# Routing noise loaded into its place, the ranking of unit 0 in later chunks, and another order of the second layer's products

## The chip, the cores and the metric

The kernel runs on one core of one Trainium2 chip. The metric is the device time of one execution in microseconds; the median of three runs is compared.

## The reference

Two blocks follow each other. First a gated linear attention over 4 x 8 heads of 768 steps with 48 features, then a router that sends each of the 3072 tokens (384 features) to 2 of 8 experts:

```python
for t in range(S):                                  # per batch and head
    state = alpha[t][:, None] * state + outer(k[t], v[t])
    y[t] = q[t] @ state
x = y, heads side by side                           # (3072, 384)
noisy = x @ w_gate + log1p(exp(x @ w_noise)) * noise
top2 = the two largest of the 8; w = softmax over the two
for e in range(8):                                  # w1[e] 384x1024, w2[e] 1024x384
    out[rows of e] += w * (relu(x[rows] @ w1[e]) @ w2[e])
```

All of it is in 32-bit floating point.

## The kernel before

**Chunks.** The attention runs over 24 chunks of 128 tokens, six to a batch entry. The main loop over n writes the order of the work out by hand: one iteration issues 15 pieces, which are numbered by place. Place 0 issues loads on SP (values of chunk n+2, alpha of n+5, keys and queries of n+4) and the store of chunk n-2. Then come keys (1), inverses (2), alphas (3), turn_y (4), turn_k (5), scaled (6), queries (7), block (8), output (9), no_more (10), state (11), scores (12), masked (13) and products (14). They belong to different chunks: keys, inverses, scaled and queries to n+2, alphas and products to n+3, turn_k, state, scores and masked to n+1, output and block to n, turn_y to n-1. Every engine works its own instructions off in that order.

**What hangs together in a chunk.** TensorE transposes keys and alphas (L347), turns the output rows (L281), turns the keys (L438, left out ahead of the last chunk of a batch entry), transposes the queries (L347), and multiplies output (L470, L258), state (L453) and scores (L426). All transposes share two banks in turn (the pool `tp`), so a transpose waits until the tile two before it has been copied out. ScalarE copies out keys, alphas, rows, blocks and outputs (L474). VectorE scans the running products (L375, tile `P_all`, one buffer) and the inverses (L387, tile `over`, one buffer), multiplies the queries (L415) and masks the scores (L431). GpSimd multiplies the keys (L405, `scaled`), copies the last column of `P_all` (L416, in the piece queries) and scales the state (L456). A new `P_all` is written only after the copy L416 of the one before.

**Routing.** A unit is six chunks; there are four. `routing` is a generator whose steps are s1 logits and exp, s2 ln, s3 the noise multiplied in (L706), s4 to s6 the two largest of two chunks each (L711, L712), with the choice and the exponential of the gates behind s6 (L729), s7 the rest of the choice and the running counts (L735 to L758, mostly GpSimd), s8 the ranks (TensorE, L763, L764), s9 the places of the table's entries. `ROUTE[u]` lists when the step is taken: (d, place) of unit u is the iteration n = d + 6(u + 1) - 1. So (3, 8) of unit 0 is n = 8 and (3, 13) of unit 1 is n = 14. Step s9 queues twelve entries, and the last thing of each iteration, `put_some(3)`, issues three of them as indirect DMAs on GpSimd (L172). The routing of units 2 and 3 lies in the second phase.

**Noise.** The noise (3072 x 8) is loaded by one DMA on SP as 24 rows of 4 KB (L236), turned by eight transposes on TensorE in iteration 2 (L242) and copied by ScalarE into its place (L243).

**Pairs.** The second phase takes 24 pairs of 128-row tiles, a pair belonging to one expert. Each has 11 products of the first layer (L1219) and 7 of the second (L1226), with sums of blocks on VectorE (`hx`, `wt`) that save products. Steps carry a time; they are sorted by it. The table of rows is read (`tab`, SP) after the entries of units 0 and 1 have been put, then the rows are gathered (L950, GpSimd). `ending` holds the end of a pair, `last_ending` that of the last. The results C and D share one bank, A and B have their own; D is `hs[1][1]` times `wt[3]`, C is `hs[1][0]` times a block of the weights, B starts with `hx[0]` times `wt[0]`.

Of the kernel before, what the change touches and what calls it, by code (L numbers as in the profile page):

```python
# [9 lines left out]
F32 = mybir.dt.float32  # L10
# [9 lines left out]
def kernel(  # L20
# [32 lines left out]
    nc = tc.nc  # L53
    B, H, S, D = q.shape
    N, DM = out.shape
    E, _, F = moe_w1.shape
    C = 128
# [173 lines left out]
                out=to_rows.rearrange("p (j o) c -> p j o c", o=2)[:, :, odd, ds((1 - odd) * 2 * D, 2 * E)],  # L231
                in_=w_r.rearrange("p (j o) w e -> p j o (w e)", o=2)[:, :, odd])

    def load_noise(on):
        by_chunk = on["two"].tile([C, KO * F], F32, tag="w1", name="by_chunk")[0:NT, 0:C * E]
        nc.sync.dma_start(out=by_chunk, in_=moe_noise.rearrange("(n p) e -> n (p e)", p=C))  # L236
        return by_chunk.rearrange("n (p e) -> n e p", e=E)

    def turn_noise(by_chunk, on):
        tp = on["tp"].tile([C, E, NT], F32, tag="tp", name="tp")  # L240
        for e in range(E):
            nc.tensor.transpose(tp[:, e, :], by_chunk[:, e, :], ident[0:NT, 0:NT])  # L242
        nc.scalar.copy(noise.rearrange("p n e -> p e n"), tp)  # L243


    def few(on, shape, name, late=False):
# [51 lines left out]
    def fast_gla(on):  # L298
# [184 lines left out]

        ROUTE = (((1, 8), (2, 8), (2, 10), (2, 11), (3, 4), (3, 8), (3, 10), (4, 12), (5, 0)), ((1, 9), (2, 8), (2, 10), (3, 1), (3, 4), (3, 11), (3, 13), (5, 0), (5, 11), (5, 12)))
        routes = [routing(u, on) for u in range(NU)]

        def route(n, place):
# [570 lines left out]
    def pairs(on):  # L1060
# [161 lines left out]
        def product2(name, H, W, new=False):  # L1222
            if new:
                open_bank(name)
            for f in range(FO // 2):
                nc.tensor.matmul(bank[name], H[:, f, :], W[:, f, :], start=new and f == 0, stop=True,  # L1226
                                 skip_group_check=True)
# [8 lines left out]
        def scaled(i, s, half, name):  # L1236
            nc.scalar.activation(o[:, s, half], bank[name], AF.Copy, scale=gate(i, s))  # L1237

        def added(i, s, half, name, to=None):
            to = o if to is None else to  # L1240
            nc.vector.scalar_tensor_tensor(to[:, s, half], bank[name], gate(i, s), to[:, s, half], op0=ALU.mult, op1=ALU.add)  # L1241
# [62 lines left out]
        def steps(i):  # L1304
# [36 lines left out]
                (10.0, lambda: less(hx[3], hs[1][0], hx[1])),  # L1341
                (10.1, lambda: less(hx[2], hs[0][0], hs[0][1])),
                (10.55, lambda: product2("A", hs[0][0], v(0, 0), True)),
                (11.9, lambda: product2("B", hx[0], wt[0], True)),
                (11.95, lambda: scaled(i, 0, LEFT, "A")),
                (13.2, lambda: product2("C", hs[1][0], v(1, 0), True)),
                (13.25, lambda: scaled(i, 1, RIGHT, "B")),
                (14.6, lambda: product2("A", hx[1], wt[1])),
                (15.95, lambda: scaled(i, 0, RIGHT, "A")),
                (6.5 if i == 5 else 8.5 + late + after, lambda: get_prev(i)),  # L1350
# [1 line left out]

        def ending(i, v, summing):
            return (
                (15.9, lambda: product2("D", hs[1][1], wt[3])),
                (17.3, lambda: product2("B", hx[3], v(1, 1))),
                (17.35, lambda: (added(i, 0, LEFT, "C"), scaled(i, 1, LEFT, "D"))),
                (18.6, lambda: product2("A", hx[2], wt[2])),
                (18.65, lambda: added(i, 0, RIGHT, "B")),
                (20.0 - 0.05, lambda: added_to_both(i, 1, "A")),  # L1360
                (summing, lambda: combine(i)),
                (summing + 1.3, lambda: put_pair(i)))

        def last_ending(i, v, summing):
            rows = prev[i % 2]
            return (
                (14.7, lambda: added(i, 0, LEFT, "C")),
                (15.9, lambda: product2("B", hx[3], v(1, 1))),
                (16.0, lambda: with_prev(i, 1, RIGHT)),
                (17.3, lambda: product2("A", hx[2], wt[2])),  # L1370
                (17.35, lambda: (added(i, 0, RIGHT, "B"), with_prev(i, 0, BOTH), put_half(i, 0))),
                (18.6, lambda: product2("D", hs[1][1], wt[3])),
                (18.65, lambda: (scaled(i, 1, LEFT, "A"), added(i, 1, RIGHT, "A", rows), with_prev(i, 1, LEFT))),
                (20.0, lambda: added(i, 1, LEFT, "D", rows)),
                (20.0, lambda: put_half(i, 1)))
# [103 lines left out]
    with ExitStack() as es:  # L1479
# [31 lines left out]
                work.pop(0)[1]()  # L1511

        held = []
        NOISE_AT = 5
        FIRST_ORDER = "scores masked inverses keys scaled turn_k queries output block state alphas no_more turn_y products"
        ORDER = "keys inverses alphas turn_y turn_k scaled queries block output no_more state scores masked products"

# [4 lines left out]
        with tc.manual_schedule():  # L1522
# [28 lines left out]
            alphas(2)  # L1551
            no_more(1)
            load(4, "a")
            held.append(load_noise(on))
            state(0)
            products(2)
            no_more(2)
            for n in range(LAST):
                pieces = {"keys": lambda: keys(n + 2), "inverses": lambda: inverses(n + 2),
                          "scaled": lambda: scaled_keys(n + 2), "alphas": lambda: alphas(n + 3),  # L1560
                          "turn_y": lambda: turn_y(n - 1), "turn_k": lambda: turn_k(n + 1),
                          "queries": lambda: queries(n + 2), "products": lambda: products(n + 3),
                          "no_more": lambda: no_more(n + 3), "block": lambda: block(n), "output": lambda: output(n),
                          "state": lambda: state(n + 1), "scores": lambda: scores(n + 1),
                          "masked": lambda: masked(n + 1)}
                names = (FIRST_ORDER if n == 0 else ORDER).split()
                assert sorted(names) == sorted(pieces)
                pieces = [lambda: (load_v(n + 2), load(n + 5, "a"), load(n + 4, "kq"), put_y(n - 2))] + \
                    [pieces[name] for name in names]
                chunk = [lambda piece=piece, place=place: (piece(), route(n, place)) for place, piece in enumerate(pieces)]  # L1570
                last = [lambda: put_some(3)]
                if n == 0:
                    chunk.append(lambda: place_router(held.pop(0)))
                if n == 1:
                    last.append(lambda: held.append(nothing_in(on["two"])))
                if n == 2:
                    chunk.append(lambda: clear_table(held.pop()))
                if n == 2:
                    last.append(lambda: (clear_pairs(), clear_halves()))
                if n == 3:  # L1580
                    last.append(place_slots)
                if n == 2:
                    chunk.insert(NOISE_AT, lambda: turn_noise(held.pop(0), on))
                for at, place, t in ((16, 9, -410.0), (15, 9, -409.0), (14, 9, -408.0), (8, 9, -405.0), (7, 9, -404.0), (6, 9, -403.0), (5, 9, -402.0), (3, 9, -300.0), (2, 1, -199.0), (1, 1, -101.0), (1, 14, -100.5), (1, -1, -100.0)):
                    if n == LAST - at:
                        chunk.insert(place, lambda t=t: until(t))
                for piece in chunk + last:
                    piece()
# [46 lines left out]
```

## Time and profile before

| | |
|---|---|
| median of 3 runs | 653.38 us (653.23 to 654.1) |
| profiled execution | 653.14 us, of which the span from the first to the last instruction is 651.1 us |
| TensorE (matmul), VectorE, ScalarE, GpSimd busy | 98%, 71%, 48%, 47% of the span |
| granted TensorE clock | 0.997 of full speed |

In a timeline a row is one or several merged instructions: start, duration, engine, line, operation, tiles, count, and in brackets how long the engine was idle before it and who ended that. Ends of matmuls are modelled, so what a stretch of TensorE cost is read from the distance of starts. The chunk of iteration n begins with the eight transposes of L347 (keys, alphas); iteration 2 begins at 29.07 us, iteration 8 at 66.94 us, iteration 16 at 118.36 us.

### The profile page before, as it was taken

To read this page: it belongs to the slowest core of one execution; us is meant where nothing else is said; L and a number is where in the kernel's file an instruction comes from. 1 tells how busy PE (TensorE), PEld (TensorE's weight loads), DVE (VectorE), ACT (ScalarE), POOL (GpSimd) and SP (SyncE) were. 2 spreads that over 40 slices of the span, in tenths; PEclk is the share of its full clock that TensorE was granted. 3 is DMA by queue.
4 is the path that set the end of the run, shared out by engine and by line. 5 is a ranking of instruction groups with operands and counts; after the bars stand their busy time and mean duration, and the time that the engine had idled before them with its cause. 6 is when DMAs were issued, how large, how long until landed. Compare 5 with 4: busy or idle time off the path is not lost. (4 is left out here: it accounts for less than half of the span.)

```text
span 651.1 us, 14753 instructions
## 1 busy us (share of the span) xinstructions
PE 637.3 (98%) x5509; PEld 614.4 (94%) x5509; DVE 461.0 (71%) x1045; ACT 310.9 (48%) x624; POOL 309.1 (47%) x407
## 2 busy tenths in 40 slices
PE   8999999999999999999999999999999999999994
PEld 6899999998999999999999999999999999998894
DVE  6778889887779888777677777567574665746532
ACT  3767778675554454433434433434334444334430
POOL 6362577784343577774353542513445044450231
PEclk9999999999999999999999999999999999999998
DMA  9999998973766676665366298943899439993011
GB/s 140 173 213 161 231 190 160 222 160 109 244 191 218 204 214 197 205 220 119 87 168 173 83 223 235 209 151 89 215 260 221 145 109 215 260 264 103 32 53 46
DMA packets 170260, 112.52 MB, mean 173 GB/s; under 512 B 135095, under 2 KB 157362, under 8 KB 170180
## 3 DMA queue, kind: packets, MB, share of 16 engines
q1 hardware_dynamic: 132340, 33.20, 30.0%
q10 hardware_dynamic: 26112, 54.30, 27.7%
q0 software_dynamic: 11728, 23.99, 12.6%
q8 instruction: 46, 0.75, 0.5%
q14 instruction: 34, 0.28, 0.1%
HBM read 95.09 MB, written 15.37 MB: 170 GB/s over the span
## 5 line engine op out<-in xcount | busy, mean ns | idle before, releaser
L942 POOL DMA_INDIRECT out_dram<-prev,where x48 | 58.1, 1210 | 164.5 <-DVE prev L1254 144.2
L1219 PE MATMUL sc<-xs,ws 128*128 128x128 f32 x576 | 78.2, 279 | 0.0
L1230 ACT ACTIVATE h<-h 128x512 f32<-128x512 f32 x72 | 45.2, 631 | 66.3 <-DVE h L1163 63.4
L1219 PE MATMUL sc<-xt,w 128*128 128x128 f32 x576 | 75.1, 275 | 0.5 <-ACT xt L1152 0.5
L950 POOL DMA_INDIRECT x_in<-x_rows,where x48 | 52.4, 1091 | 44.7 <-issue 29.1
L1219 PEld LDWEIGHTS sc<-xt,w 128*128 128x128 f32 x576 | 70.5, 192 | 0.8 <-ACT xt L1152 0.8
L1219 PEld LDWEIGHTS sc<-xs,ws 128*128 128x128 f32 x576 | 70.0, 192 | 0.8 <-issue 0.2
L1226 PE MATMUL o_ps<-wt,hx 128*128 128x192 f32 x384 | 70.2, 326 | 0.0
L931 POOL DMA_INDIRECT prev<-out_dram,where x48 | 52.1, 1085 | 36.2 <-DMA out_dram<-prev_half,where_half 16.6
L1163 DVE TENSOR_TENSOR h<-sc,m 128x512 f32<-128x512 f32 x48 | 33.2, 691 | 47.1 <-PE sc L1219 44.4
L1226 PEld LDWEIGHTS o_ps<-wt,hx 128*128 128x128 f32 x384 | 63.7, 190 | 0.0
L172 POOL DMA_INDIRECT table<-entry,place_u x48 | 54.2, 1130 | 15.2 <-issue 12.1
L1219 PE MATMUL h_ps<-xt,w 128*128 128x128 f32 x384 | 50.7, 275 | 0.0
L1237 ACT ACTIVATE o<-o_ps,tab 128x192 f32<-128x192 f32 x49 | 20.6, 420 | 59.2 <-PE o_ps L1226 58.5
L1241 DVE SCALAR_TENSOR_TENSOR o<-h_ps,tab,o 128x192 f32<-128x192 f32 x48 | 20.0, 416 | 38.9 <-PE h_ps L1226 38.2
L1219 PE MATMUL sc<-xs,w 128*128 128x128 f32 x384 | 46.8, 275 | 0.0
L1219 PEld LDWEIGHTS h_ps<-xt,w 128*128 128x128 f32 x384 | 46.7, 192 | 0.0
L405 POOL TENSOR_TENSOR k_P<-k_P,over 128x512 f32<-128x512 f32 (+1 forms) x25 | 28.9, 1159 | 37.2 <-DVE over L387 31.5
L347 PE MATMUL tp<-ident,ins 128*128 128x128 f32 x288 | 44.3, 290 | 1.6 <-DMA ins<-in_alpha_dram 0.5
L1219 PEld LDWEIGHTS sc<-xs,w 128*128 128x128 f32 x384 | 44.8, 192 | 0.0
L347 PEld LDWEIGHTS tp<-ident,ins 128*128 128x128 f32 x288 | 33.5, 148 | 6.7 <-issue 1.6
L1237 ACT ACTIVATE o<-h_ps,tab 128x192 f32<-128x192 f32 x47 | 19.9, 422 | 39.8 <-DVE o L1241 31.1
(262 smaller groups left out, 1442.7 us busy)
## 6 DMA issues: line engine op xcount, KB each, us to landing
w<-in_moe_w_dram ACTq DMA_DIRECT2D x42, 512.0 KB
w<-in_moe_w_dram ACTq DMA_DIRECT2D x56, 384.0 KB
ins<-in_alpha_dram SPq DMA_DIRECT2D x24, 192.0 KB
ins<-in_k_dram SPq DMA_DIRECT2D x24, 192.0 KB
ins<-in_q_dram SPq DMA_DIRECT2D x24, 192.0 KB
vt<-in_v_dram SPq DMA_DIRECT2D x24, 192.0 KB
x_rows<-y_sb SPq DMA_DIRECT2D x24, 192.0 KB
ins<-in_moe_w_dram ACTq DMA_DIRECT2D x9, 512.0 KB
```

The lines of the kernel that those rows point to most:

```text
L172: put = nc.gpsimd.indirect_dma_start(out=table, out_offset=bass.IndirectOffsetOnAxis(ap=place, axis=0), in_=entry, in_offset=None, bounds_ ...
L347: nc.tensor.transpose(tp[:, j, :], src[:, 2 * j:2 * j + 2, :], ident)
L405: nc.gpsimd.tensor_tensor(c["k"][:, at], c["k"][:, at], over[:, at, 1:CB], op=ALU.mult)
L931: get = nc.gpsimd.indirect_dma_start(out=rows.bitcast(U32), out_offset=None, in_=out.bitcast(U32), in_offset=bass.IndirectOffsetOnAxis(ap= ...
L942: put = nc.gpsimd.indirect_dma_start(out=out, out_offset=bass.IndirectOffsetOnAxis(ap=at, axis=0), in_=rows, in_offset=None, bounds_check= ...
L950: nc.gpsimd.indirect_dma_start(out=rows, out_offset=None, in_=x_rows[0:units * UT, :], in_offset=bass.IndirectOffsetOnAxis(ap=at, axis=0), ...
L1163: nc.vector.tensor_tensor(to, p, q, op=ALU.add)
L1219: nc.tensor.matmul(bank[name][:, f, :], W[:, ds(f * C, C)], X, start=new and f == 0, stop=True, skip_group_check=True)
L1226: nc.tensor.matmul(bank[name], H[:, f, :], W[:, f, :], start=new and f == 0, stop=True, skip_group_check=True)
L1230: nc.scalar.activation(t, t if src is None else src, AF.Relu)
L1237: nc.scalar.activation(o[:, s, half], bank[name], AF.Copy, scale=gate(i, s))
L1241: nc.vector.scalar_tensor_tensor(to[:, s, half], bank[name], gate(i, s), to[:, s, half], op0=ALU.mult, op1=ALU.add)
```

## The change

Three parts. The noise is loaded per unit by four DMAs of 768 runs of 32 bytes straight into its tile, in iterations 3, 8, 13 and 18, behind place 0; the transposes and the copy are gone. In `ROUTE`, steps s6 to s9 of unit 0 move one iteration later, and step s4 of unit 1 moves from place 1 of iteration 14 to place 11 of iteration 13. In a pair the order of the second layer's products A, B, C, A, D, B, A becomes A, D, B, A, C, B, A: D now opens the bank that it shares with C, and the scaling of B's first half is 1.4 later. The last pair keeps the old order.

```diff
-    def load_noise(on):
-        by_chunk = on["two"].tile([C, KO * F], F32, tag="w1", name="by_chunk")[0:NT, 0:C * E]
-        nc.sync.dma_start(out=by_chunk, in_=moe_noise.rearrange("(n p) e -> n (p e)", p=C))
-        return by_chunk.rearrange("n (p e) -> n e p", e=E)
-
-    def turn_noise(by_chunk, on):
-        tp = on["tp"].tile([C, E, NT], F32, tag="tp", name="tp")
-        for e in range(E):
-            nc.tensor.transpose(tp[:, e, :], by_chunk[:, e, :], ident[0:NT, 0:NT])
-        nc.scalar.copy(noise.rearrange("p n e -> p e n"), tp)
+    def load_noise(u):
+        nc.sync.dma_start(out=noise[:, ds(u * UC, UC)], in_=moe_noise[ds(u * UT, UT), :].rearrange("(n p) e -> p n e", p=C))
...
-        ROUTE = (((1, 8), (2, 8), (2, 10), (2, 11), (3, 4), (3, 8), (3, 10), (4, 12), (5, 0)), ((1, 9), (2, 8), (2, 10), (3, 1), (3, 4), (3, 11), (3, 13), (5, 0), (5, 11), (5, 12)))
+        ROUTE = (((1, 8), (2, 8), (2, 10), (2, 11), (3, 4), (4, 8), (4, 10), (5, 12), (6, 0)), ((1, 9), (2, 8), (2, 10), (2, 11), (3, 4), (3, 11), (3, 13), (5, 0), (5, 11), (5, 12)))
...
-                (11.9, lambda: product2("B", hx[0], wt[0], True)),
                 (11.95, lambda: scaled(i, 0, LEFT, "A")),
-                (13.2, lambda: product2("C", hs[1][0], v(1, 0), True)),
-                (13.25, lambda: scaled(i, 1, RIGHT, "B")),
...
         def ending(i, v, summing):
             return (
-                (15.9, lambda: product2("D", hs[1][1], wt[3])),
+                (11.9, lambda: product2("D", hs[1][1], wt[3], True)),
+                (13.2, lambda: product2("B", hx[0], wt[0], True)),
+                (14.65, lambda: scaled(i, 1, RIGHT, "B")),
+                (15.9, lambda: product2("C", hs[1][0], v(1, 0))),
...
         def last_ending(i, v, summing):
             return (
+                (11.9, lambda: product2("B", hx[0], wt[0], True)),
+                (13.2, lambda: product2("C", hs[1][0], v(1, 0), True)),
+                (13.25, lambda: scaled(i, 1, RIGHT, "B")),
...
-        NOISE_AT = 5
+        NOISE_AT = (3, 8, 13, 18)
...
-            held.append(load_noise(on))
...
-                if n == 2:
-                    chunk.insert(NOISE_AT, lambda: turn_noise(held.pop(0), on))
+                if n in NOISE_AT:
+                    chunk.insert(1, lambda: load_noise(NOISE_AT.index(n)))
```

## Rows read from the trace of the kernel before

**Rows 1.** Page, part 1: busy time, share of the span, instructions.

```profile
PE 637.3 (98%) x5509; PEld 614.4 (94%) x5509; DVE 461.0 (71%) x1045; ACT 310.9 (48%) x624; POOL 309.1 (47%) x407
```

**Rows 2.** Groups by line, TensorE: count, busy us, mean ns, idle before it.

```profile
L1226 PE MATMUL h_ps<-wt,hx 128*128 128x192 f32 x192 | 35.2, 326 | 0.0
```

**Rows 3.** Timeline of TensorE, iterations 2 and 3: start, us, what.

```profile
29.07 1.09 PE L347 MATMUL tp<-ident,ins 128*128 128x128 f32 x8
30.98 1.06 PE L242 MATMUL tp<-ident,by_chunk 24*128 24x24 f32 x8
36.67 1.09 PE L347 MATMUL tp<-ident,ins 128*128 128x128 f32 x8
42.91 1.09 PE L347 MATMUL tp<-ident,ins 128*128 128x128 f32 x8
```

**Rows 4.** Page, part 3: a DMA queue's packets, MB, share of 16 engines; then TensorE's waits.

```profile
q1 hardware_dynamic: 132340, 33.20, 30.0%
PE tp L347 <- DMA ins<-in_alpha_dram: 0.5, 1, 0.5
```

**Rows 5.** Timeline of TensorE, iterations 9 and 10.

```profile
73.17 1.09 PE L347 MATMUL tp<-ident,ins 128*128 128x128 f32 x8
74.59 1.15 PE L281 MATMUL h_ps<-to_rows,yT 128*128 128x112 f32 x8 [0.34 <-ACT yT L474]
80.22 0.42 PE L763 MATMUL h_ps<-chosen,before 128*128 128x48 f32 x2
80.70 1.06 PE L347 MATMUL tp<-ident,ins 128*128 128x128 f32 x8
```

**Rows 6.** Timeline of ScalarE, iterations 8 and 9.

```profile
73.84 0.23 ACT L729 ACTIVATE entry<-entry 128x12 f32<-128x12 f32 x1 [1.56 <-DVE entry L723]
79.69 0.72 ACT L463 COPY S_block<-S 64x192 f32<-64x192 f32 x2 [2.25 <-POOL S L456]
```

**Rows 7.** Timeline of GpSimd, iteration 15, and of VectorE, iterations 15 and 16.

```profile
118.29 1.19 POOL L405 TENSOR_TENSOR k_P<-k_P,over 128x512 f32<-128x512 f32 x1
119.42 0.19 POOL L416 COPY P_end<-P_all 128x4 f32<-128x4 f32 x1
119.64 1.52 DVE L375 TENSOR_TENSOR_SCAN P_all<-shared,least 128x516 f32<-128x516 f32 x1 [0.59 <-POOL P_end L416]
122.56 0.66 DVE L415 TENSOR_TENSOR q_P<-tp,P_all 128x512 f32<-128x512 f32 x1
```

**Rows 8.** GpSimd from 86.5 to 122.5 us: the puts by line, then timeline rows.

```profile
L172 POOL DMA_INDIRECT table<-entry,place_u x12 | 14.3, 1190 | 3.2 <-issue 3.0 <-POOL S L448 0.2
98.75 0.51 POOL L456 TENSOR_TENSOR S<-S,P_end 128x192 f32<-128x192 f32 x1 [0.30 <-DVE S L455]
...
103.32 1.21 POOL L405 TENSOR_TENSOR k_P<-k_P,over 128x512 f32<-128x512 f32 x1
...
108.58 1.70 POOL L172 DMA_INDIRECT table<-entry,place_u  x1 [0.30 <-issue]
```

**Rows 9.** Timeline of TensorE, iterations 15 and 17.

```profile
113.10 0.63 PE L438 MATMUL tp<-ident,k_P 128*128 128x128 f32 x4 [0.20 <-ACT k_P L397]
...
123.91 1.07 PE L347 MATMUL tp<-ident,ins 128*128 128x128 f32 x8
```

**Rows 10.** Timeline ahead of the first pair: GpSimd, VectorE, GpSimd, TensorE.

```profile
146.24 1.17 POOL L172 DMA_INDIRECT table<-entry,place_u  x1 [0.31 <-issue]
152.33 0.17 DVE L1117 TENSOR_SCALAR tab<-tab 128x2 f32<-128x2 f32 x1 [0.75 <-DMA tab<-table]
153.12 1.83 POOL L950 DMA_INDIRECT x_in<-x_rows,where  x1 [3.90 <-DVE where L1128]
160.31 1.16 PE L1219 MATMUL sc<-xt,w 128*128 128x128 f32 x8 [0.54 <-ACT xt L1152]
```

**Rows 11.** Timeline of TensorE, one pair.

```profile
551.20 1.54 PE L1226 MATMUL h_ps<-wt,hx 128*128 128x192 f32 x8
552.58 1.46 PE L1226 MATMUL h_ps<-w,h 128*128 128x192 f32 x8
```

## The prediction

> **What bounds the kernel now.** I read the page first: TensorE's matmuls are busy 98% of the span [rows 1], so a change counts if it takes work from TensorE or changes one of the few places where it waits. The groups by line show where it doesn't wait: the second layer's product that starts B has no idle time ahead of its 192 matmuls [rows 2], and the others look the same. What is left is the chunk phase, where the distance between the first transposes of successive iterations is what an iteration costs. An undisturbed one takes 42.91 - 36.67 = 6.24 us; iteration 2, which turns the noise, takes 36.67 - 29.07 = 7.60 [rows 3]. So I go through the chunk phase queue by queue, and ask of each moved step who is behind it.
>
> **Noise, the gain.** The eight transposes and the copy behind them make iteration 2 longer by 7.60 - 6.24 = 1.36 us [rows 3]. Nothing else of that iteration is late, so all of it should go: -1.36. The lower end is what the eight transposes alone show as busy, 1.06, the upper end 1.4.
>
> **Noise, the cost.** Four loads of 768 packets join SP's queue. The queue's 132340 packets took 30.0% of 16 engines' span of 651.1 us, which is 23.6 ns for one, of 251 bytes in the mean [rows 4]; 768 of them over 16 engines are at most 1.13 us a load. TensorE waited for an input load only at the start, 0.5 us [rows 4], and a load is issued about two iterations, 12 us, before its use; that is the cover, so I take 0. Without it four loads would cost 4 x 1.13 = 4.5. The Trainium skill speaks against such loads (DMA: Bandwidth & Descriptors, the section Measured (HBM→SBUF, 128 partitions, SWDGE, issued from GpSimd)): below 64 KB the count of descriptors decides, at about 10.5 ns a packet. By that a load would be an estimated 0.5 us of the engines, and the sum stays the same as long as the cover holds. SP's issue is one more instruction behind place 0; TensorE, VectorE and ScalarE don't wait for it. The two pieces of weight loading that the insertion moves by one place are SP's too: 0.
>
> **Unit 0, iteration 9.** Iteration 9 takes 80.70 - 73.17 = 7.53 us, of which 80.70 - 80.22 = 0.48 are the rank products and 7.53 - 6.24 - 0.48 = 0.81 are waits, the largest for ScalarE's output copy yT [rows 5]. The cause is one iteration earlier: the gates' exponential of step s6 waits 1.56 us on ScalarE for VectorE, and yT is behind it [rows 6]. With s6 one iteration later, VectorE has only two of the six maxima in each iteration and should reach the gates before TensorE needs yT. The wait goes: -0.81. What is late next: the running counts of s7 (GpSimd) now end in iteration 10, and behind them the scaled state and ScalarE's block copy. That copy was 2.25 us late in iteration 9 before [rows 6]. Iteration 10 has no turned keys and is shorter, so yT of iteration 10 comes out just when it is needed in iteration 11, and the next transposes wait some 0.3 for copies. I take -0.81 + 0.3 = -0.5, with the ends 0 and -0.81. The rank products only change their iteration: 0.
>
> **Unit 0, its puts.** This is the costly part, and it isn't visible in the diff. Step s9 goes from iteration 10 to 11, so the four groups of three puts end iterations 11 to 14 instead of 10 to 13. In iteration 14 unit 1 has its s7, whose counts on GpSimd are last. Before, iteration 14 had no puts, and the scaled keys of the next iteration start right after the counts, at 118.29 [rows 7]. Now a group stands between them. Twelve puts cost 14.3 + 3.2 us, that is 17.5 / 4 = 4.37 a group [rows 8]. The shortest group, from the end of the state's scaling at 98.75 + 0.51 = 99.26 to 103.32, is 4.06; with one put of 1.70 in place of 1.19 it would be 4.9 [rows 8]. I take the mean, since it is the same work on the same queue.
>
> Who waits: behind the puts stand the scaled keys (1.19) and the copy of the last column of `P_all`, which ends at 119.42 + 0.19 = 119.61. VectorE already waits 0.59 us for that copy before it may write the next `P_all` [rows 7]. So VectorE is late by the whole 4.37. Its scans lead to the multiplied queries, which now end at 122.56 + 0.66 = 123.22 [rows 7]. The alphas' transposes of iteration 17 need that bank; they are the second half of the eight that begin at 123.91, so at about 124.36 [rows 9]. The margin is 124.36 - 123.22 = 1.14, and TensorE loses 4.37 - 1.14 = 3.2 us there.
>
> The rest of the 4.37 comes due at the first pair. Unit 1's four groups of puts follow in GpSimd's queue behind the same late inverses, the last ends at 146.24 + 1.17 = 147.41, and from there a chain of waits runs to the first product: the table's read lands and ends VectorE's idle 0.75 at 152.33, GpSimd's gather has waited 3.90 for VectorE's row numbers, and TensorE waits 0.54 for the turned rows at 160.31 [rows 10]. This chain is last there already, so it carries all 4.37 to the pairs: +4.4.
>
> **Unit 1's step s4.** It moves ahead of the masks and scans of iteration 13 in VectorE's queue, but the gates of s6 still have the same work ahead of them. The wait of iteration 15 (0.20 idle and a few tenths around it [rows 9]) stays: 0, at best -0.4.
>
> **Second layer.** The product that starts B takes 552.58 - 551.20 = 1.38 us in one pair instead of 1.30 [rows 11], which is a wait for `hx[0]` of 0.08. With D in its place the wait has 1.3 us more room. `hs[1][1]` and `wt[3]` are made long before. C's sum waited for the whole bank before, that is for D in the fifth place, and now for C in the fifth place: no change. B's scaling comes 1.3 later but has two products until B is written again. So -0.1 in all, and 0 in the other pairs, since TensorE has no wait there to lose [rows 2].
>
> **The sum.** -1.36 - 0.5 + 4.4 + 0 - 0.1 = +2.4. On the profiled execution's own 653.14 us (span 651.1 and 2.04 around it) this is 655.5; the median lies 0.24 above that execution, so 655.8. With all ends one way the forecast itself spans 4.06 - 1.4 - 0.81 - 0.4 - 0.1 = +1.3 to 4.9 - 1.06 - 0 = +3.8, or 654.7 to 657.2.
>
> **Rivals.** (a) The later puts are hidden, and the gains stay: -1.36 - 0.5 - 0.1 = -2.0, 651.4, faster. Place: GpSimd between iterations 14 and 15. It decides if a group delays the scaled keys by less than the margin of 1.14 us. For it speaks that GpSimd is busy only 47% of the span [rows 1]; against it the copy that VectorE already waits for [rows 7]. Chance 0.12. (b) TensorE loses its 3.2 but the chain at the first pair gives the difference back, because puts run faster beside a waiting VectorE or VectorE catches up: 3.2 - 1.36 - 0.5 - 0.1 = +1.2, 654.6, no change that can be told. Chance 0.18. (c) The new order in the pairs makes TensorE wait where it doesn't now, for a bank or a copy that I follow wrongly; at the 0.08 of the one wait that there is, 23 pairs lose 1.8 on top: 657.6. Chance 0.05. (d) The noise loads are not covered, because the input loads run out of lead: 4.5 on top, 660.3; the single 0.5 us wait for a load speaks against it [rows 4]. Chance 0.03. By the Trainium skill's figure above the uncovered loads would be an estimated 4 x 0.5 = 2.0 on top.
>
> **How the numbers follow.** The forecast has 0.62. A measurement of this kernel tells about 0.2% from no change, 1.3 us, so no change is 652.1 to 654.7. Faster is (a): 0.12. No change is most of (b) and the edges: 0.16. Slower is the rest, 0.72. The range leaves out (a) and (d), and with the tails no more than 2 in 10: 653.3 to 657.8.
>
> **What would show it.** Right: iteration 2 as long as iteration 3; three puts on GpSimd right behind the counts of unit 1, the next scaled keys some 4.4 us later against TensorE, VectorE idle over 4 us before the following `P_all`, two waits of TensorE of together about 3 us in iterations 16 and 17; the first product of the pairs some 2.5 us later than 160.31; pair lengths unchanged. Wrong: an iteration 16 of the old length, or waits of TensorE for DMA in the chunk phase, or pairs that are longer or shorter by a tenth each.

## The result, and the profile after

The changed kernel takes 656.58 us, the median of 11 runs (654.9 to 658.57); the kernel before takes 653.29 beside it (11 runs, 651.71 to 654.1). The ratio is 1.0054, with the interval [1.0044, 1.0064]: slower by about 3.5 us. The forecast was 655.8. The profiled execution of after has 658.57 us and a span of 656.7, the slowest of its eleven. Its span is 5.6 longer than that of before (651.1), where the medians differ by 3.3; so a term read from this one trace can be larger than its share of the median.

The page, part 1 (busy time) and the row of part 2 with the clock granted to TensorE in 40 slices:

```profile
PE 639.9 (97%) x5501; PEld 616.9 (94%) x5501; DVE 460.9 (70%) x1045; ACT 312.4 (48%) x623; POOL 310.2 (47%) x407
PEclk9999999899999999999999999999999999999998
```

TensorE has eight matmuls fewer and is busy 2.6 us more [rows 1]. The 8 in the eighth slice is the first hint of why: between 115 and 131 us the granted clock isn't full. In before that digit is a 9.

TensorE's waits in after (line, who released it: us in total, times, longest):

```profile
PE tp L339 <- DVE q_P L407: 1.8, 1, 1.8
...
PE sc L418 <- POOL k_P L397: 1.3, 2, 1.1
...
PE tp L339 <- DMA ins<-in_alpha_dram: 0.5, 1, 0.5
```

The first two are new. The wait for an input load is the 0.5 us that was there before [rows 4], so the noise loads cost TensorE nothing that shows; they landed 2.9 to 3.7 us after their issue.

Cut into iterations (distance from the eight transposes that begin one to those that begin the next, worked out from the timelines of both), the 138.56 us from the start of iteration 1 to the first product of the pairs in before, and the 143.38 in after, lie like this. Iterations that aren't named have 6.23 in both, but for 1 and 4, which are as long in after as in before.

| iteration | 2 | 9 | 10 | 11 | 15 | 16 | 17 | last stretch, to the pairs | sum |
|---|---|---|---|---|---|---|---|---|---|
| before | 7.60 | 7.53 | 5.31 | 6.23 | 7.44 | 5.55 | 6.21 | 11.50 | 138.56 |
| after | 6.23 | 6.23 | 5.82 | 6.60 | 7.58 | 6.67 | 11.14 | 11.91 | 143.38 |
| difference | -1.37 | -1.30 | +0.51 | +0.37 | +0.14 | +1.12 | +4.93 | +0.41 | +4.82 |

From there to the end it is 490.97 us in after and 490.76 in before. Of the other 0.8 of the 5.6, 0.6 lies ahead of iteration 1, which starts at 22.38 instead of 21.75; the kernels of the experiments start it between 20.14 and 22.24, whatever was changed.

**The gains.** TensorE of after, the first transposes of iterations 2, 3 and 4 (as [rows 3]), then of 9, 10, 11 and 12 (as [rows 5]); start, duration, what:

```profile
29.70 1.09 PE L339 MATMUL tp<-ident,ins 128*128 128x128 f32 x8
...
35.93 1.09 PE L339 MATMUL tp<-ident,ins 128*128 128x128 f32 x8
...
42.16 1.09 PE L339 MATMUL tp<-ident,ins 128*128 128x128 f32 x8
```

```profile
72.42 1.09 PE L339 MATMUL tp<-ident,ins 128*128 128x128 f32 x8
...
78.65 1.09 PE L339 MATMUL tp<-ident,ins 128*128 128x128 f32 x8
...
84.47 1.06 PE L339 MATMUL tp<-ident,ins 128*128 128x128 f32 x8
...
91.07 1.09 PE L339 MATMUL tp<-ident,ins 128*128 128x128 f32 x8
```

Iteration 2 is as long as iteration 3. Iteration 9 has lost its waits and its rank products, iteration 10 has the rank products now, and iteration 11 is 0.37 longer.

**The puts.** GpSimd of after, iteration 15: the end of unit 1's counts, the three puts, the scaled keys and the copy of the last column (as [rows 7]):

```profile
117.11 0.20 POOL L750 TENSOR_TENSOR seen<-past,chosen 128x8 f32<-128x8 f32 x1
117.83 1.02 POOL L172 DMA_INDIRECT table<-entry,place_u  x1 [0.52 <-issue]
119.15 0.98 POOL L172 DMA_INDIRECT table<-entry,place_u  x1 [0.30 <-issue]
120.44 0.98 POOL L172 DMA_INDIRECT table<-entry,place_u  x1 [0.30 <-issue]
121.43 1.19 POOL L397 TENSOR_TENSOR k_P<-k_P,over 128x512 f32<-128x512 f32 x1
122.55 0.19 POOL L408 COPY P_end<-P_all 128x4 f32<-128x4 f32 x1
```

From the end of the counts (117.31) to the scaled keys (121.43) the group takes 4.12. VectorE stands meanwhile:

```profile
122.78 1.52 DVE L367 TENSOR_TENSOR_SCAN P_all<-shared,least 128x516 f32<-128x516 f32 x1 [4.75 <-POOL P_end L408]
...
125.70 0.67 DVE L407 TENSOR_TENSOR q_P<-tp,P_all 128x512 f32<-128x512 f32 x1
```

**What TensorE makes of it.** Its timeline from the start of iteration 16 (117.34) over that of 17 (124.01) to that of 18 (135.16):

```profile
117.34 1.06 PE L339 MATMUL tp<-ident,ins 128*128 128x128 f32 x8
...
119.55 1.06 PE L462 MATMUL y<-q_P,S_block 128*128 128x128 f32 x8
120.54 1.09 PE L250 MATMUL y<-shared,vt 128*48 128x128 f32 x16
122.68 1.16 PE L418 MATMUL sc<-q_P,k_P 48*128 48x128 f32 x16 [1.05 <-POOL k_P L397]
...
124.01 0.63 PE L339 MATMUL tp<-ident,ins 128*128 128x128 f32 x4
126.42 1.11 PE L339 MATMUL tp<-ident,ins 128*128 128x128 f32 x4 [1.77 <-DVE q_P L407]
127.33 1.89 PE L273 MATMUL h_ps<-to_rows,yT 128*128 128x112 f32 x8
...
130.71 1.91 PE L462 MATMUL y<-q_P,S_block 128*128 128x128 f32 x8
132.56 1.12 PE L250 MATMUL y<-shared,vt 128*48 128x128 f32 x16
...
135.16 1.09 PE L339 MATMUL tp<-ident,ins 128*128 128x128 f32 x8
```

The two waits that the forecast named are there. But behind the second one no wait follows, and the work still takes nearly twice as long: the output product of iteration 16 runs from 119.55 to 120.54, that of iteration 17 from 130.71 to 132.56, 1.85 for the same eight matmuls. The windows show it. A row has the stretch and its length, then for TensorE's matmuls, its weight loads, VectorE, ScalarE and GpSimd the busy us and the instructions, then the granted clock, the share of the DMA engines and their GB/s. First after, then before over the first two of these stretches:

```profile
117.00:125.80 8.80, 6.51 (x68) 5.78 (x68) 3.98 (x6) 4.49 (x11) 4.97 (x8) 1.00 0.80 167
125.84:132.67 6.83, 6.25 (x30) 6.03 (x32) 5.96 (x13) 2.67 (x7) 5.92 (x9) 0.50 0.86 174
132.70:139.00 6.30, 6.30 (x84) 6.00 (x86) 4.03 (x6) 4.19 (x11) 4.32 (x6) 1.00 0.67 114
```

```profile
117.00:125.80 8.80, 8.67 (x95) 7.99 (x92) 7.90 (x17) 5.42 (x14) 5.54 (x14) 1.00 0.94 195
125.84:132.67 6.83, 6.83 (x88) 6.53 (x87) 5.97 (x9) 4.92 (x14) 5.79 (x7) 1.00 1.05 220
```

For 6.83 us the granted clock is 0.50, the lower of its two levels (1.2 instead of 2.4 GHz), and TensorE gets 30 matmuls done where before had 88 (in part others, and shorter ones). Ahead of it TensorE was busy 6.51 of 8.80 us. Iteration 17 is 4.93 longer than in before; its wait put off the second half of the transposes from 124.48 (0.47 behind the first, as where there is no wait) to 126.42, 1.94; so 4.93 - 1.94 = 2.99 is put down to the low clock; the experiment with three spare products tests it.

**At the pairs.** TensorE at the first pair of after, then GpSimd's last put ahead of it and its gather (as [rows 10]), then one pair's products A, D and B (as [rows 11]):

```profile
165.76 1.16 PE L1211 MATMUL sc<-xt,w 128*128 128x128 f32 x8 [0.42 <-ACT xt L1144]
```

```profile
151.27 1.17 POOL L172 DMA_INDIRECT table<-entry,place_u  x1 [0.30 <-issue]
...
158.57 1.83 POOL L942 DMA_INDIRECT x_in<-x_rows,where  x1 [4.33 <-DVE where L1120]
```

```profile
556.92 1.46 PE L1218 MATMUL h_ps<-wt,h 128*128 128x192 f32 x8
558.22 1.46 PE L1218 MATMUL h_ps<-wt,hx 128*128 128x192 f32 x8
```

The first product is 5.45 later on the axis than the 160.31 of before. From the start of the gather to it, it is 165.76 - 158.57 = 7.19, as in before (160.31 - 153.12 [rows 10]). D in the second place takes 558.22 - 556.92 = 1.30, so the wait of 0.08 that B had there [rows 11] is gone.

### The profile page after: what moved, and what is told of

Its sections match the earlier page's. It is cut to its first block, busy times and chain, and to the rows that moved or that the text cites. A ratio compares the mean times of both kernels' runs of the same rounds, so it can differ in the third digit from the quotient of the medians.

```text
span 656.7 us, 14751 instructions
## 1 busy us (share of the span) xinstructions
PE 639.9 (97%) x5501; PEld 616.9 (94%) x5501; DVE 460.9 (70%) x1045; ACT 312.4 (48%) x623; POOL 310.2 (47%) x407
## 5 line engine op out<-in xcount | busy, mean ns | idle before, releaser
L339 PE MATMUL tp<-ident,ins 128*128 128x128 f32 x288 | 45.8, 296 | 3.3 <-DVE q_P L407 1.8
L423 DVE COPY_PREDICATED shared<-upto,sc 128x512 f32<-128x512 uint32 x48 | 32.4, 730 | 7.2 <-PE sc L418 7.1
```

The lines of the kernel that those rows point to most:

```text
L339: nc.tensor.transpose(tp[:, j, :], src[:, 2 * j:2 * j + 2, :], ident)
L423: nc.vector.copy_predicated(MTs[n % 2][:, i], mask_upto, sc)
```

## Experiments

Three theories stood against each other: that the time is lost by the group of puts in iteration 14 and by nothing else of the change; that the noise or the order of the products costs some of it; and, for the size, that the low clock behind the waits is an item of its own, and not just another face of late data. The kernels noise alone (first run), order alone (first run), unit 0 alone and the one with all three puts in iteration 15 were timed together where the kernel before took 671.02 us; in the traces of these four it is 501.56 to 514.92 us from the first product of the pairs to the end, where after has 490.97. Three spare products ran where the kernel before took 681.57. For these the chunk phase is compared and the time only against its own neighbour. The distance is always that from iteration 1 to the first product of the pairs: 138.56 in before, 143.38 in after. It doesn't tell small differences: order alone, run again, has the iterations of before to within 0.01 us and yet a last stretch of 11.00 instead of 11.50.

**Noise alone.**

```diff
...
-        NOISE_AT = 5
+        NOISE_AT = (3, 8, 13, 18)
...
-                if n == 2:
-                    chunk.insert(NOISE_AT, lambda: turn_noise(held.pop(0), on))
+                if n in NOISE_AT:
+                    chunk.insert(1, lambda: load_noise(NOISE_AT.index(n)))
```

> The kernel before with the noise loads alone. Theory (the eight transposes were all on TensorE's path, the four loads are covered): iteration 2 takes 6.24 us instead of 7.60, nothing else moves, so 1.36 us less than before: ratio 0.998, about 651.9. Rival (the loads of 32-byte runs take the lead of the input loads): TensorE waits for loads behind iterations 3, 8, 13 and 18, up to 1.1 us each, and the time is that of before or longer: 653.3 to 656.

Measured: 670.41 against 671.02, ratio 0.9992 [0.9957, 1.0027], too wide to tell. Iteration 2 takes 6.23, the distance is 137.29, 1.27 less. So I ran it again where the pairs weren't disturbed:

> The kernel before with the noise loads moved into place 1 and nothing else, on a chip where the weights in the pairs come in time. The trace of its first run had iteration 2 at 6.23 instead of 7.60 and the distance to the pairs 1.27 shorter, so if that reaches the end the time is 1.3 below the kernel before, ratio 0.998; the rival, that it is given back before the pairs or in them, has 1.000.

Measured: 651.82 against 653.1, ratio 0.9977 [0.9967, 0.9988]; distance 137.08. By the medians the 1.3 us arrive at the end of the kernel. The trace can't show that: its execution is the slowest of the twelve (653.55), with a wait of TensorE of 1.53 in the pairs that before doesn't have. This kernel has the lowest median of all here, and it beats both the one before and the one after.

**Order of the second layer's products alone.**

```diff
-                (11.9, lambda: product2("B", hx[0], wt[0], True)),
-                (13.2, lambda: product2("C", hs[1][0], v(1, 0), True)),
-                (13.25, lambda: scaled(i, 1, RIGHT, "B")),
...
-                (15.9, lambda: product2("D", hs[1][1], wt[3])),
+                (11.9, lambda: product2("D", hs[1][1], wt[3], True)),
+                (13.2, lambda: product2("B", hx[0], wt[0], True)),
+                (14.65, lambda: scaled(i, 1, RIGHT, "B")),
+                (15.9, lambda: product2("C", hs[1][0], v(1, 0))),
...
```

> The kernel before with the order A, D, B, A, C, B, A of the second layer alone. Theory: TensorE has no wait in the pairs to lose but 0.08 us in one, so no change: 653.2, ratio 1.000, the distance from the first product of the pairs to the end unchanged to 0.2 us. Rival: the new order makes each pair wait for a bank or a copy, 23 times 0.08 us or more: 655.1 or longer.

Measured: ratio 1.0009 [0.9977, 1.0040]. And where the pairs weren't disturbed:

> The kernel before with the new order of the second layer's products once more, beside the others of this call, for the pairs: theory 0, at best 0.1 us less than before; rival 1.8 us more.

Measured: 653.03 against 652.93, ratio 1.0003 [0.9994, 1.0013]; from the first product to the end 491.0 (before: 490.76). The order is worth nothing that can be told, in either direction.

**Unit 0 alone: s6 to s9 one iteration later.**

```diff
-        ROUTE = (((1, 8), (2, 8), (2, 10), (2, 11), (3, 4), (3, 8), (3, 10), (4, 12), (5, 0)), ...
+        ROUTE = (((1, 8), (2, 8), (2, 10), (2, 11), (3, 4), (4, 8), (4, 10), (5, 12), (6, 0)), ...
```

> The kernel before with steps s6 to s9 of unit 0 one iteration later alone. Theory: this part carries the whole loss. TensorE waits about 1.1 us in iteration 16 and 1.9 in iteration 17, the granted clock then falls to half for some 6 us, iteration 9 loses its 0.8 us of waits and iteration 11 gains 0.4: the changed kernel's time plus the 1.4 us of the noise, 657.9, ratio 1.007. Rival (the loss needs the noise loads or the new order of products as well): below 656, ratio under 1.004.

Measured: 676.31 against 671.02, ratio 1.0083 [1.0049, 1.0117]. The waits of iterations 16 and 17 are those of after to within 0.02, and so are the slow matmuls behind them (TensorE, this kernel; four transposes take 1.11 where the four ahead of the wait took 0.63):

```profile
123.25 1.16 PE L426 MATMUL sc<-q_P,k_P 48*128 48x128 f32 x16 [1.07 <-POOL k_P L405]
...
124.58 0.63 PE L347 MATMUL tp<-ident,ins 128*128 128x128 f32 x4
127.00 1.11 PE L347 MATMUL tp<-ident,ins 128*128 128x128 f32 x4 [1.78 <-DVE q_P L415]
```

The granted clock is 0.50 for 6.83 us from 126.5 on, as long as in after. Iterations 16 and 17 take 6.69 and 11.17, the distance is 143.77. Up to the start of iteration 21 it is 132.77, in after 131.46: 1.31 more, which is the noise's gain. The ratio of after, 1.0054, and the noise's gain of 0.0023 (the second run above) make 1.0077, which lies in this interval, wide as it is. So this part carries the loss; the noise, the order and step s4, which are as in before here, are not needed for it.

**The group of puts taken out of iteration 14.** The changed kernel, with the three puts a group later:

```diff
-                last = [lambda: put_some(3)]
+                last = [lambda: put_some(0 if n == 14 else 3)]
```

> The changed kernel with the last three puts of unit 0 at the end of iteration 15 instead of 14, nothing else. Theory: the scaled keys of iteration 15 start right behind the counts again, the waits of iterations 16 and 17 and the low clock behind them go. The puts fall into GpSimd's 2.7 us of idle time ahead of the scaled keys of iteration 16, which come 1.65 us late and with them unit 1's puts and the first pair: -1.36 - 0.5 - 0.1 + 1.65 = -0.3 against before, 653.0. Rival (the loss comes from elsewhere in the later ranking): the time stays at the changed kernel's 656.6.

Measured: the time (671.08 against 671.02) says nothing, since the pairs were disturbed here most of all. The chunk phase does (TensorE of this kernel, from the scores of iteration 16 into iteration 17):

```profile
121.03 1.16 PE L418 MATMUL sc<-q_P,k_P 48*128 48x128 f32 x16
...
122.37 1.07 PE L339 MATMUL tp<-ident,ins 128*128 128x128 f32 x8
```

No wait ahead of the scores, the eight transposes in one run. Iterations 16 and 17 take 5.55 and 6.97, the granted clock is 1.00 in the whole chunk phase, and the distance is 137.34: 6.0 less than after. The 1.65 that I expected back at the first pair didn't come: the last stretch is 11.00. So it is this group, in this iteration, and not a later step as such.

**One put of the three left in iteration 14.**

```diff
-                last = [lambda: put_some(3)]
+                last = [lambda: put_some(1 if n == 14 else 3)]
```

> The changed kernel with one put of unit 0 instead of three at the end of iteration 14 and the other two at the end of 15: the dose. Theory (GpSimd's queue decides, with 1.14 us of margin): one put delays the scaled keys by 1.4 to 1.5 us, TensorE waits 0.2 to 0.5 us in iterations 16 and 17, the clock stays, and from iteration 1 to the first product it takes 137.3 to 138 us. Rival (any put in that place costs the whole wait, or the clock): over 139 us.

Measured: 653.2 against 652.93, ratio 1.0009 [1.0000, 1.0017]; distance 138.98, more than I expected. The wait of iteration 16 and the low clock are gone, and of the wait of iteration 17 0.35 is left, within the 0.2 to 0.5 expected (iterations 16 and 17: 5.55 and 6.87). Behind it iterations 18 to 20 take 19.28 together instead of 18.69, and the last stretch 12.29 instead of 11.50. TensorE comes earlier to the first pair, and the rows don't (TensorE in iteration 17 and at the first pair, then GpSimd, this kernel):

```profile
121.75 0.66 PE L339 MATMUL tp<-ident,ins 128*128 128x128 f32 x4 [0.35 <-DVE q_P L407]
...
159.21 1.16 PE L1211 MATMUL sc<-xt,w 128*128 128x128 f32 x8 [0.54 <-ACT xt L1144]
```

```profile
152.00 1.84 POOL L942 DMA_INDIRECT x_in<-x_rows,where  x1 [2.59 <-DVE where L1120]
```

Counted from the start of iteration 1 the gather starts at 131.77 here and at 131.37 in before: later by 0.40, as the distance is by 0.42. The chain that the forecast called last at the first pair is last here. Here it takes back what noise and iteration 9 had gained.

**Spare products, first form.** To part the low clock from the wait, products that nothing reads fill TensorE's two waits in the changed kernel:

```diff
+        def fill(times):
+            for _ in range(times):
+                nc.tensor.matmul(few(on, [C, C], "fill"), ident, ident, start=True, stop=True)
...
-                          "scaled": lambda: scaled_keys(n + 2), "alphas": lambda: alphas(n + 3),
+                          "scaled": lambda: scaled_keys(n + 2), "alphas": lambda: (fill(8 if n == 17 else 0), alphas(n + 3)),
...
-                          "state": lambda: state(n + 1), "scores": lambda: scores(n + 1),
+                          "state": lambda: state(n + 1), "scores": lambda: (fill(5 if n == 16 else 0), scores(n + 1)),
```

> The changed kernel with 5 spare products of 128 columns ahead of the scores in iteration 16 and 8 ahead of the alphas in iteration 17, where TensorE waited 1.05 and 1.78 us; nothing reads their results. Theory (the wait is 3.1 us, and the idle TensorE then lost its clock, which doubled the cost of what followed): the clock stays at full speed, iteration 17 shrinks from 11.14 to about 8.2 us, and from the first transposes of iteration 1 to the first product of the pairs it takes 140.4 to 141.2 us instead of 143.4; the time falls by 2 to 3 us. Rival (the clock fell for another reason, or the products behind the wait were slow for another reason): the distance stays 143.4 or grows by what the spare products delay.

Measured: 662.18 against 652.93, ratio 1.0136 [1.0118, 1.0153]. The test was spoilt, because the bank I chose holds the ranks until VectorE has read them (TensorE of this kernel, iteration 16):

```profile
126.45 2.08 PE L1519 MATMUL h_ps<-ident 128*128 128x128 f32 x8 [4.54 <-DVE picked L761]
```

Instead of filling the wait the spare products made it 4.54 us, and the granted clock was 0.50 for 10.2 us from 125.7 on. It says nothing on a filled wait, only that here a longer one came with a longer stretch at the lower level.

**Spare products into a free bank.** The same two places, but into the bank of the state's product, which has no reader then:

```diff
-                nc.tensor.matmul(few(on, [C, C], "fill"), ident, ident, start=True, stop=True)
+                nc.tensor.matmul(on["o"].tile([C, DM], F32, name="o_ps")[:, 0:C], ident, ident, start=True, stop=True)
```

> The changed kernel with spare matrix products that nothing reads, into the bank of the state's product, which is free at that time and waits for nothing: five before the scores of iteration 16 and eight before the transposes of the log-decays of iteration 17, where TensorE stood 1.05 and 1.78 us in the changed kernel. (The same idea went into the bank of the rank before, and waited there.) Theory that the low granted clock behind those waits is an item of its own: it stays at full speed, the waits themselves remain (iteration 16 about 6.7, iteration 17 about 6.2 + 1.9 = 8.1 instead of 11.14), and from iteration 1 to the first product of the pairs it is 140.4 to 141.6 instead of 143.38: ratio to the kernel before 1.001 to 1.004. Rival, that iteration 17 is long because its data comes late and the clock only shows the idleness: iteration 17 stays at about 11, the distance at 143.4, the ratio at 1.005.

Measured: 658.06 against 653.1, ratio 1.0074 [1.0062, 1.0087], distance 143.06. The clock stayed at 1.00, so that half of the theory held; but the time did not come, because the spare products were longer than the waits: eight took 4.21 us, 0.53 each, where four of the output product take 0.99 (119.55 to 120.54 above), and the five ahead of the scores took 2.67. With those in the way, neither theory is told apart by the time.

> As the one with spare products ahead of both waits, but only the eight ahead of the second (iteration 17); the wait of 1.05 us in iteration 16 stays idle. If the second wait is the one behind which the clock falls, it stays at full speed and the time is that of the kernel with both filled (distance 140.4 to 141.6); if the first wait suffices, the clock falls all the same, earlier, and iterations 16 and 17 together are about 17.8 as in the changed kernel (6.67 + 11.14), distance about 143.4.

Measured (only the eight ahead of the second wait): 656.42 against 653.1, ratio 1.0054 [1.0039, 1.0069]; distance 141.76, just above the 140.4 to 141.6 expected. TensorE of this kernel, from the scores of iteration 16 on (PEld: its weight loads):

```profile
122.16 1.16 PE L418 MATMUL sc<-q_P,k_P 48*128 48x128 f32 x16 [1.05 <-POOL k_P L397]
...
123.96 4.21 PE L1519 MATMUL o_ps<-ident 128*128 128x128 f32 x16
124.41 0.30 PEld L1519 LDWEIGHTS o_ps<-ident 128*128 128x128 f32 x2 [0.25 <-PE o_ps L1519]
...
128.01 0.60 PE L339 MATMUL tp<-ident,ins 128*128 128x128 f32 x4
128.45 1.04 PE L273 MATMUL h_ps<-to_rows,yT 128*128 128x112 f32 x8
```

The wait of 1.05 stays idle and the clock stays full (the rows product takes 1.04, in after 1.89). So the first wait alone doesn't bring the clock down here; whether the second alone would was not tried. Iterations 16 and 17 take 6.67 and 10.26 together with some 2.3 us of spare work beyond the wait. The row of weight loads shows why the spare work is long: each product's weight load stands 0.25 us until the product before it, which writes the same tile, has ended.

**Three spare products.**

```diff
-                          ... "alphas": lambda: (fill(8 if n == 17 else 0), alphas(n + 3)),
+                          ... "alphas": lambda: (fill(3 if n == 17 else 0), alphas(n + 3)),
```

> The kernel with spare products ahead of the second wait only, three of them instead of eight. In that run eight took 4.21 us, 0.53 each, where the wait was 1.78: the clock stayed at full speed, and iterations 16 and 17 took 6.67 and 10.26, of which about 2.3 us was spare work beyond the wait. Three take 1.6 us and lie within the wait. Theory that the low granted clock is an item of its own: it stays at full speed, iterations 16 and 17 take 6.67 and 8.1, the distance to the first product of the pairs is 139.4 to 140.4 instead of 143.38, and the ratio to the kernel before is 1.001 to 1.003. Rival, that any shorter filling lets the clock fall again, or that something else then ends late: distance 142 to 143.4, ratio 1.004 to 1.005.

Measured: the time (685.93 against 681.57) is that of a disturbed second phase, without a ratio. The chunk phase (TensorE, and GpSimd's last put ahead of the gather):

```profile
122.28 1.48 PE L1519 MATMUL o_ps<-ident 128*128 128x128 f32 x6
124.22 0.66 PE L339 MATMUL tp<-ident,ins 128*128 128x128 f32 x4 [0.46 <-DVE q_P L407]
124.71 1.04 PE L273 MATMUL h_ps<-to_rows,yT 128*128 128x112 f32 x8
...
147.11 1.16 POOL L172 DMA_INDIRECT table<-entry,place_u  x1 [0.30 <-issue]
```

The spare work lies inside the wait, 0.46 of it is left, and the clock stays full. Iterations 16 and 17 take 6.68 and 8.21, where after has 6.67 and 11.14: 2.93 us less. The data is as late as in after: counted from the start of iteration 1 (20.14 here) the second half of the transposes of iteration 17 starts at 104.08, in after at 104.04. The distance is 140.53, 0.13 above the span I gave, and 0.93 of it lies in iteration 19, which takes 7.16 us in this run; most of that is a stop of TensorE within the scores of that iteration, for which the profile shows no releaser. The rival that the data is late anyway has fallen: the data is as late and iteration 17 is not as long. How much of these 2.9 us the end of the kernel would keep isn't shown, for want of an undisturbed time.

**Unit 0's s6 behind the output copy of the same iteration, with the noise.** The wait of iteration 9 was to go without any puts moving:

```diff
-        ROUTE = (((1, 8), (2, 8), (2, 10), (2, 11), (3, 4), (3, 8), (3, 10), (4, 12), (5, 0)), ...
+        ROUTE = (((1, 8), (2, 8), (2, 10), (2, 11), (3, 4), (3, 10), (3, 10), (4, 12), (5, 0)), ...
```

> The kernel before with the noise loads and with step s6 of unit 0 at place 10 of iteration 8 instead of 8, so that ScalarE's wait for the gates stands behind the output copy and no_more; all else of the ranking as before. Theory: iteration 9 loses its 0.8 us of waits without any put being moved, iteration 2 its 1.37: 138.56 - 1.37 - 0.8 = 136.4 us from iteration 1 to the first product, and a time 2.1 us below before, ratio 0.997. Rival (the wait only moves to the keys' copy behind the gates): half of the 0.8 stays, 136.8 us, ratio 0.9975.

Measured: 652.12 against 652.93, ratio 0.9987 [0.9978, 0.9996]. Faster than before, but not faster than the noise alone (0.9977). The distance is 137.70, where 136.4 was expected and 136.8 by the rival: both missed. Iteration 9 falls from 7.53 to 7.07, and iteration 10 rises from 5.31 to 6.17 (TensorE of this kernel, iteration 10):

```profile
80.16 1.15 PE L273 MATMUL h_ps<-to_rows,yT 128*128 128x112 f32 x8 [0.32 <-ACT yT L466]
```

The late copy of yT has only moved into the next iteration, where it costs more.

## Why the prediction was right, and where its sum was not

**Noise, right.** -1.36 was forecast, -1.37 measured, and it reaches the end (ratio 0.9977 alone). The loads are covered: no new wait for a DMA. The cover is longer than the 12 us of the prediction: the load of iteration 3 is issued at 40.31 and first read at 65.58. What an uncovered load costs no run here shows. The prediction's estimate of 0.5 us a load from the Trainium skill (DMA: Bandwidth & Descriptors, the section Measured (HBM→SBUF, 128 partitions, SWDGE, issued from GpSimd)) is less sure than it looks: the section has 10.5 ns a packet for a transfer of 64 packets that takes 0.67 us, and doesn't say that this is the time of one of 16 engines. Taken as the time of the whole transfer it would make an estimated 8.1 us of 768 packets. Landing took 2.9 to 3.7 us from the issue.

**Unit 0, iterations 9 to 11, right.** Forecast -0.81, with 0.3 of it given back in iteration 11. Iterations 9 to 11 changed by -1.30 + 0.51 + 0.37 = -0.42, of which the rank products only moved from 9 to 10; iteration 11 gave back 0.37. Forecast -0.5.

**The puts: place, order and size right.** A group of 4.37 was forecast between counts and scaled keys, at least 4.06; it is 4.12. VectorE stands 4.75 us for the copy, over 4 as forecast. The two waits put TensorE back by 1.12 + 1.94 = 3.06, forecast 3.2.

**The low clock, missed.** Nothing in the forecast has it. In before the granted clock is 1.00 in every stretch around this place, so no row showed a price, and I took the waits for the whole loss. TensorE stood from 121.63 to 122.68 and from 124.65 to 126.42; at 125.84, within the second wait, the clock fell to its lower level for 6.83 us, and 2.99 us went there. Filling part of the second wait brings back 2.93 in that iteration. This is the term that the sum lacked.

**The remainder at the first pair: the chain right, its size in the sum not.** +1.2 was to come on top of TensorE's own loss, as the chain from the last put to the gather was to be late by the whole group. The chain is last in after as it was in before: 7.19 us from the gather to the first product in both. Counted from the start of iteration 1 the last put ends 4.40 later than in before (130.06 instead of 125.66) and the gather starts 4.82 later. But the 4.40 is not what the forecast added up, from which 1.36 and 0.5 were still to go. With three spare products, where the clock stays full, the last put ends at 128.13 (147.11 + 1.16 - 20.14), so some 1.9 of the 4.40 came with the low clock. As TensorE itself was late by 1.12 + 1.94 + 2.99 = 6.05, only +0.41 is left for the last stretch, which is no more than the 0.5 by which that stretch differs between two runs with the same iterations. The chain's length isn't steady either: from the end of the last put to the gather it takes 5.71 in before, 6.13 in after, 4.84 with three spare products and 4.40 with one put in iteration 14. So this term could not be known to better than a microsecond.

**Step s4 and the second layer, right.** Forecast 0 and -0.1. Iteration 15, where a gain of up to 0.4 had room, takes 7.58 instead of 7.44; s4's move was not tried by itself. The 0.08 in one pair went, and the order alone is 1.0003.

**The sum.** Forecast +2.4. By terms in the trace: noise -1.37, iterations 9 to 11 -0.42, waits +3.06, iteration 15 +0.14, clock +2.99, last stretch +0.41, which is +4.81 of the 4.82. The median moved by 3.3, nearer to the forecast than the profiled execution. Seven of the eleven runs of after have a granted clock of 0.991, and a mean of 657.43 us; four have 0.993 and a mean of 655.75. It may be that the clock term is smaller in the four, but that isn't shown: only one of the eleven has a trace, and in the kernel before the runs at 0.995 and those at 0.997 don't differ in time (652.93 and 653.06 in the mean, beside the second run of order alone). So 655.8 came near 656.58 with a term of 2.99 missing and one of 1.2 that measured 0.41. The direction, the place and the waits were right; that the sum came this near is in part luck.

**The rivals.** (a) fell: the puts are not hidden; the margin of 1.14 us against 4.12. (b), that the chain gives the difference back, fell in after, where the chain was last and 4.82 late. At the full clock it is open: with three spare products the first product is 1.97 later than in before, between the 1.2 of (b) and the forecast's 2.4, and the chain is no longer last (7.55 from the gather to the first product). (c) and (d) fell, by the order alone and by the waits.

**What the Trainium skill says of this.** TensorE: Matmul & The Clock Gate, section A second HAM failure mode: psum-queue depth-cycling, tells of a kernel in which frequent short idle times between groups of matmuls let the clock swing between its two levels, with the loss paid between the bursts. The trace agrees in part: the clock fell during the second of two short waits, and 2.99 us were lost behind it. But here it fell once, without waits that recur, and the loss lies in matmuls that ran at the lower level.

## What to carry to other kernels

When a step with DMA issues is moved on a queue, list what else that queue has in the new iteration; one group of puts of 4.1 us in a queue that is busy 47% cost more than both real gains of the change. When a kernel keeps TensorE busy without a break, price a new wait not by its length alone: look at the granted clock behind it. Where a wait can't be avoided, independent products that are due anyway would be the filling; that was not tried here, only spare ones. And time the parts of a change by themselves: here one part alone is a gain of 0.23%, and all together a loss of 0.54%.

## What the runs showed of the hardware

- The granted clock fell to 0.50 in the middle of a phase that had run at 1.00 for 109 us, during the second of two idle times of 1.05 and 1.77 us, and was full again 6.83 us later, TensorE having worked all of that but the first 0.6. With 4.54 us of idleness it stayed low for 10.2 us. Where only 1.05, or 1.06 and 0.46, were left, it did not fall.
- A spare product takes 4.21 / 8 = 0.53 us, where the output product, at the same shape, takes 0.99 / 4 = 0.25. The trace shows the cause: all spare products write the same tile, and the weight load of each stands 0.25 us until the product before it has ended.
- Three indirect DMAs in a row took 4.12 us of GpSimd's queue in after, where their spans are 1.02 + 0.98 + 0.98 = 2.98; a group priced by its spans alone would have been over a quarter too cheap.
